# Two heads' key-value products in one chain of matmuls

## The chip, the cores and the metric

The kernel runs on one core of one Trainium2 chip. The metric is the device time of one execution in microseconds, from the median of several runs. The kernel before takes 1669.48 us (median of 3 runs, 1668.96 to 1672.15).

## What is computed

Linear attention with an RMS norm, and two MLPs behind it, all in float32 in and out. For each of 8 batches and 8 heads (576 positions, 64 channels):

```python
kv = np.einsum('bhsd,bhse->bhde', k, v)
out = np.einsum('bhsd,bhde->bhse', q, kv)
rms = np.sqrt(np.mean(out * out, axis=-1, keepdims=True) + 1e-06)
attn = out / rms * g_norm
x = attn.transpose(0, 2, 1, 3).reshape(4608, 512)
h = x @ moe_w_in;   x = np.where(h >= 1, h, np.where(h <= -1, 0, (h + 1)**2 / 4)) @ moe_w_out
h = x @ moe2_w_in;  x = np.maximum(h, 0)**2 @ moe2_w_out
```

The MLPs are 512 to 2048 to 512 wide. The change is in the first line alone: the product of the keys with the values, a 64 x 64 matrix for each head, summed over 576 positions.

## The kernel before

The work goes in blocks of 512 tokens. TensorE's product of two float32 numbers split in a high and a low part (three matmuls in the float32r format, `mm3`, L190) makes both MLPs accurate; the first MLP runs over 9 blocks of 16 hidden slices (`h_stage`, `g_stage`, `out_stage`), the second works on pairs of blocks with fewer products (L688), from about 850 us on. The main loop is a list of steps, one for each hidden slice; a table of hooks puts other work between the halves of a step: the loads and splits of the first MLP's weights during block 0, and the attention of the batch that the next block needs (`attention`, `load_kv`, `load_q`). Batch 0's attention runs ahead of all MLP work. The program's builder orders the queues of the engines from this; the order on an engine isn't always the code's.

The heads are taken in pairs, 4 pairs for each batch, 32 in all. For a pair, `load_kv` brings 512 of the 576 positions of the keys and of the values into a tile of 128 partitions x 512 numbers each: partition p holds positions 4p to 4p + 3 (L342 to L347). Both tiles are laid out head by head, so that the four positions of one head and one partition are one run of 1 KB. The last 64 positions of each head, the rest, go into a tile of their own with 64 partitions (L349, L350 for batches 1 to 7; for batch 0 all heads at once, L382). All these loads are issued by SyncE (SP), in one queue, together with those of queries, weights and outputs.

`kv_stage` (L388 on) then multiplies: for head 0 four float32 matmuls over 128 positions each and one over the rest, accumulated in one bank in rows and columns 0 to 63; then the same for head 1 in rows and columns 64 to 127. A float32 matmul is issued to TensorE as two pairs of a weight load and a matmul, so a pair of heads takes 20 matmul instructions: 16 of L395 (128 rows, 64 columns of weights, 64 columns moved) and 4 of L396 (64 rows). The bank's two diagonal blocks are then copied out, for batch 0 into `kv0`, otherwise split into `kvbd` (DVE, L171 and L404), block diagonal matrices whose other blocks stay zero. `o_stage` multiplies the transposed queries of both heads with them at once.

Of the kernel before, what the change touches and what calls it, by code (L numbers as in the profile page):

```python
# [73 lines left out]
def linear_attention_rms_two_mlps(  # L74
# [12 lines left out]
    nc = tc.nc  # L87
    B, H, S, D = q.shape
    NT, DM = out.shape
    DFF = w_in1.shape[1] // 2  # L90
    P = 128
# [4 lines left out]
    MR = TB // P  # L96
# [59 lines left out]
    def engine(op, phase):  # L156
        return engines[next(turns[op][min(phase, 2)])]
# [9 lines left out]
    def copy(e, dst, src):  # L167
        if e is nc.scalar:
            e.copy(dst, src)  # L169
        elif e is nc.vector:  # L170
            e.tensor_copy(dst, src)  # L171
        else:
            scaled(e, dst, src, 1.0)
# [149 lines left out]
    def bank(b, name):  # L323

        pool, tag = next(banks) if b == 0 else (ps_t, "at")
        return pool.tile([P, TB], F32, tag=tag, name=name)
# [9 lines left out]
    def load_kv(b, hp):  # L336
        h0 = 2 * hp
        if b > 0:
            r = ap2.tile([REM, 2, 2, D], F32, tag="rem", name=f"rem_{b}_{hp}")
            kvr[b, hp] = (r[:, 0], r[:, 1])  # L340
        for n, src in enumerate((k, v)):
            pool, tag = (ep, "e") if (b, hp) == (0, NP - 1) else (st, "st")  # L342
            t = pool.tile([P, TB], F32, tag=tag, name=f"{'kv'[n]}_{b}_{hp}")
            t = t.rearrange("p (h r d) -> p h r d", h=2, r=MR)
            rows = src[b, h0 : h0 + 2, :TB, :].rearrange("h (p r) d -> p h r d", r=MR)
            nc.sync.dma_start(t, rows)
            kvm.setdefault((b, hp), []).append(t)  # L347
            if b > 0:
                rest = src[b, h0 : h0 + 2, TB:, :].rearrange("h p d -> p h d")  # L349
                nc.sync.dma_start(kvr[b, hp][n], rest)  # L350
# [14 lines left out]
    def load_first():  # L365

        left = wp.tile([REM, 2, H, D], F32, tag="w0_3", name="kvr0")
        qr = wp.tile([REM, H, D], F32, tag="w1_3", name="qr0")
        for hp in range(NP):
            load_kv(0, hp)  # L370
            heads = slice(2 * hp, 2 * hp + 2)
            kvr[0, hp] = (left[:, 0, heads, :], left[:, 1, heads, :])
            pool, tag = (ep, "e") if hp == NP - 1 else (st, "st")
            t = pool.tile([P, TB], F32, tag=tag, name=f"q_0_{hp}")
            t = t.rearrange("p (c h d) -> p c h d", h=2, c=MR)
            for j in range(2):
                rows = q[0, 2 * hp + j, :TB, :].rearrange("(c p) d -> p c d", p=P)
                nc.sync.dma_start(t[:, :, j, :], rows)
            qs[0, hp] = [t[:, c] for c in range(MR)] + [qr[:, heads, :]]
            if hp == 0:  # L380
                for t, src in ((left[:, 0], k), (left[:, 1], v), (qr, q)):
                    nc.sync.dma_start(t, src[0, :, TB:, :].rearrange("h p d -> p h d"))  # L382
                for j in range(2):
                    nc.sync.dma_start(
                        gvec[j * D : (j + 1) * D, :], g_norm.rearrange("(d o) -> d o", o=1)
                    )

    def kv_stage(b, hp):  # L388
        kt, vt = kvm.pop((b, hp))
        r = kvr.pop((b, hp))  # L390
        ps = bank(b, f"pkv_{b}_{hp}")
        for j in range(2):
            s = slice(j * D, (j + 1) * D)
            for c in range(MR):
                nc.tensor.matmul(ps[s, s], kt[:, j, c, :], vt[:, j, c, :], start=c == 0, stop=False)  # L395
            nc.tensor.matmul(ps[s, s], r[0][:, j, :], r[1][:, j, :], start=False, stop=True)  # L396
        for j in range(2):
            s = slice(j * D, (j + 1) * D)
            if b == 0:
                copy(engine("kv_hi", b), kv0[s, hp, s], ps[s, s])  # L400
                continue
            t = kvbd[hp % len(kvbd)]
            copy(engine("kv_hi", b), t[s, 0, s], ps[s, s])
            nc.vector.tensor_tensor(t[s, 1, s], ps[s, s], t[s, 0, s].bitcast(F32), ALU.subtract)  # L404
# [73 lines left out]
    def attention(b):  # L478

        slots = {}  # L480

        def at(s, f, *a):
            slots.setdefault(s, []).append((f, a))

        def begin():
            new_x(1, b)
            xrem[b] = ap2.tile([P, KD, REM], F32, tag="xrem", name=f"xrem_{b}")

        at(0, begin)
        for hp in range(NP):  # L490
            for half in range(2):
                u = 2 * hp + half
                if half == 0:
                    at(6 * hp if b == 0 else 3 * u, kv_stage, b, hp)
                at(6 * hp if b == 0 else 3 * u, t_stage, b, hp, half)
                at(6 * hp + 5 if b == 0 else 3 * u + 2, o_stage, b, hp, half)
                at(6 * hp + 10 if b == 0 else 3 * u + 4, r_stage, b, hp, half)
        return slots
# [348 lines left out]
    for n, (L, b) in enumerate(blocks):  # L847
        nxt = blocks[n + 1] if n + 1 < len(blocks) else None
        if nxt and nxt[0] == 1 and nxt[1] < B:
            nb = nxt[1]  # L850
            for hp in range(NP):
                s = max(0, 6 * hp - 6)
                if hp > 0:
                    when = (n, s // 2)
                else:
                    when = (n, 0) if n == 0 else (n - 1, NF - 3)
                hook(*when, 0, load_kv, nb, hp)
                hook(*when, 0, load_q, nb, hp)
            hook(n, 0, 0, store_xrem, nb - 1)
            for s, fs in attention(nb).items():  # L860
                for f, a in fs:
                    hook(n, s // 2, s % 2, f, *a)
        elif nxt:
            hook(n, 0, 0, store_xrem, B - 1)
            for c in range(KD):
                hook(n, 2 + c, 0, load_x, *nxt, c)
                hook(n, 8 + c, 0, split_x, *nxt, c)
# [45 lines left out]
    ps = bank(0, "pwarm")  # L913
# [4 lines left out]
    for j in range(2):  # L918
        s = slice(j * D, (j + 1) * D)
# [100 lines left out]
```

## Time and profile before

| | |
|---|---|
| median of the runs | 1669.48 us |
| the profiled execution's own time | 1670.26 us |
| its span, first to last instruction | 1668.5 us |
| PE, matmuls | 1634.9 us busy, 98% |
| DVE, ACT | 61%, 56% busy |
| granted TensorE clock, mean of the span | 0.989 |
| DMA | 302 MB, 181 GB/s |
| instructions in the span | 21700 |

Engines are PE (TensorE's matmuls), PEld (its weight loads, which overlap PE), DVE (VectorE), ACT (ScalarE), POOL (GpSimd) and SP (SyncE, which issues the DMAs). Times in the rows are microseconds from the start of the span, if nothing else is said. Matmuls are pipelined: the shown length of one runs from its start to the modelled arrival of its last result, so that the next one begins before it ends. What a chain of matmuls costs is therefore read from start to start. L12 is line 12 of the kernel. "A <-B" behind an idle time names what ended it.

### The profile page before, as it was taken

Reading aid. Unit: us, or ns where it says so; the run is one execution under the profiler, and the core shown is the slowest. Engines: PE = TensorE matmul, PEld = TensorE weight load, DVE = VectorE, ACT = ScalarE, POOL = GpSimd, SP = SyncE. Lnnn points to the kernel's source line nnn. Section 1 sums busy time; section 2 is a strip of 40 time slices with the busy share of each in tenths; the row PEclk is TensorE's granted clock in tenths of the full one; section 3 lists DMA queues with packets and bytes.
Section 4 is the critical chain, followed back from the end, with each engine's and each line's share of the span. In section 5 each row is a group of like instructions: output and inputs, shape, how many; then the busy total and the mean of one; then the engine's idle time right before and its main releaser. Section 6 shows DMA issues by size and latency. Waiting matters only on the chain.

```text
span 1668.5 us, 21700 instructions
## 1 busy us (share of the span) xinstructions
PE 1634.9 (98%) x7640; PEld 1335.9 (80%) x7640; DVE 1009.6 (61%) x1846; ACT 936.6 (56%) x1757; POOL 111.9 (7%) x109
## 2 busy tenths in 40 slices
PE   7888999999999999999999999999999999999998
PEld 4666888888888888888888888888888878887886
DVE  5988775767767676653234346844874496447522
ACT  6775765657657565654344366545654664664321
POOL 0000000000000000000000022003101210230000
PEclk8998999999999999999999999999999999999999
DMA  8634747567574665704041356666756666665663
GB/s 258 211 121 139 239 142 240 177 185 249 163 239 148 209 188 154 242 1 155 1 138 52 113 191 225 206 222 199 241 193 224 196 236 212 207 220 188 220 195 108
DMA packets 219483, 302.37 MB, mean 181 GB/s; under 512 B 95728, under 2 KB 157168, under 8 KB 219376
## 3 DMA queue, kind: packets, MB, share of 16 engines
q1 hardware_dynamic: 219376, 301.00, 56.6%
q8 instruction: 61, 1.00, 0.2%
q14 instruction: 46, 0.38, 0.1%
HBM read 231.74 MB, written 69.21 MB: 180 GB/s over the span
## 4 chain that ended last, share of the span: by engine, by line
PE 89%; DVE 6%; ACT 2%; issue 1%; DMA 1%; SPq 0%; DVEq 0%; ACTq 0%
PE ph L190 26%; PE acc L190 25%; PE ph L688 18%; PE po L688 13%; PE pkv L395 2%; DVE t L633 2%; PE po L190 1%; PE pkv L396 1%; PE pr L454 1%; PE pt L835 1%; DMA xr<-x1d 1%; DVE x L633 1%; ACT w L169 0%; DVE d L222 0%; DVE h L741 0%
## 5 line engine op out<-in xcount | busy, mean ns | idle before, releaser
L190 PE MATMUL ph<-x,w 128*128 128x512 f32 x1728 | 427.7, 396 | 15.1 <-ACT w L169 8.5
L190 PEld LDWEIGHTS ph<-x,w 128*128 128x128 f32 x1728 | 325.7, 191 | 84.0 <-ACT w L169 12.5
L688 PE MATMUL po<-t,ws 128*128 128x512 f32 x1344 | 311.8, 391 | 2.4 <-DVE t L633 2.4
L688 PE MATMUL ph<-x,ws 128*128 128x512 f32 x1344 | 309.1, 390 | 0.0
L688 PEld LDWEIGHTS po<-t,ws 128*128 128x128 f32 x1344 | 250.2, 188 | 56.8 <-DVE t L633 5.6
L688 PEld LDWEIGHTS ph<-x,ws 128*128 128x128 f32 x1344 | 251.4, 188 | 51.9
L190 PE MATMUL acc<-gs,w 128*128 128x512 f32 x1152 | 284.9, 393 | 0.9 <-DVE gs L183 0.9
L190 PEld LDWEIGHTS acc<-gs,w 128*128 128x128 f32 x1152 | 212.1, 189 | 43.7 <-DVE gs L183 1.4
L523 ACT ACTIVATE u<-ph,halfb 128x512 f32<-128x512 f32 x144 | 99.2, 689 | 190.8 <-PE ph L190 190.3
L633 DVE TENSOR_TENSOR t<-g,t 128x512 fp32r<-128x512 f32 x192 | 134.8, 709 | 72.7 <-ACT t L169 72.7
L525 DVE SCALAR_TENSOR_TENSOR u<-u,ph 128x512 f32<-128x512 f32 x144 | 97.7, 679 | 125.9 <-ACT u L177 124.7
L169 ACT CAST t<-g 128x512 fp32r<-128x512 f32 x192 | 116.5, 621 | 72.3 <-DVE t L633 50.9
L169 ACT CAST gs<-u 128x512 fp32r<-128x512 f32 x160 | 99.4, 621 | 84.6 <-DVE u L525 72.6
L183 DVE TENSOR_TENSOR gs<-u,gs 128x512 fp32r<-128x512 f32 x160 | 110.2, 689 | 50.5 <-ACT gs L169 48.7
L190 PE MATMUL acc<-gs,wt 128*128 128x512 f32 x576 | 139.3, 391 | 0.0
L190 PEld LDWEIGHTS acc<-gs,wt 128*128 128x128 f32 x576 | 107.4, 188 | 22.4
L741 DVE TENSOR_TENSOR h<-ph,e 128x512 f32<-128x512 f32 x96 | 66.4, 691 | 63.2 <-PE ph L688 53.0
L177 ACT ACTIVATE u<-u 128x512 f32<-128x512 f32 x144 | 91.0, 633 | 1.7
L742 ACT ACTIVATE h<-h 128x512 f32<-128x512 f32 x96 | 60.7, 632 | 53.7 <-DVE h L741 48.8
L749 POOL TENSOR_TENSOR t<-g 128x512 f32<-128x512 f32 x32 | 43.1, 1347 | 649.6 <-ACT g L743 398.0
L743 ACT ACTIVATE g<-h 128x512 f32<-128x512 f32 x128 | 80.9, 632 | 3.6
L733 DVE TENSOR_TENSOR e<-ph,e 128x512 f32<-128x512 f32 x64 | 43.4, 688 | 47.0 <-PE ph L688 46.0
(101 smaller groups left out, 1619.6 us busy)
## 6 DMA issues: line engine op xcount, KB each, us to landing
ws<-wsd SPq DMA_DIRECT2D x224, 512.0 KB, 3.9
wsd<-s SPq DMA_DIRECT2D x112, 256.0 KB, 3.6
wt<-wtd SPq DMA_DIRECT2D x48, 512.0 KB, 4.0
raw<-in_moe_w_in_dram SPq DMA_DIRECT2D x32, 512.0 KB, 6.1
raw<-in_moe_w_out_dram SPq DMA_DIRECT2D x32, 512.0 KB, 5.6
wcd<-s SPq DMA_DIRECT2D x32, 512.0 KB, 3.5
ws<-wcd SPq DMA_DIRECT2D x32, 512.0 KB, 4.2
x1d<-ev SPq DMA_DIRECT2D x36, 256.0 KB, 3.6
```

What stands on the lines that cost most here:

```text
L169: e.copy(dst, src)
L177: e.activation(dst, src, AF.Square)
L183: engine(op + "_lo", phase).tensor_tensor(t[:, 1, :], src, t[:, 0, :].bitcast(F32), ALU.subtract)
L190: nc.tensor.matmul(dst, wt(a), xt(c), start=first and n == 0, stop=last and n == 2)
L523: nc.scalar.activation(u, ps, AF.Relu, bias=halfb, scale=0.5)
L525: nc.vector.scalar_tensor_tensor(u, u, 1.0, ps, op0=ALU.min, op1=ALU.max)
L633: engine2(op + "_lo").tensor_tensor(t[:, 1, :], src, t[:, 0, :].bitcast(F32), ALU.subtract)
L688: nc.tensor.matmul(ps, wt(a), xt(c), start=first and n == 0 and i == 0, stop=last and n == len(lhs) - 1 and i == 2, skip_group_check=True,)
L733: nc.vector.tensor_tensor(e[i, p], bank, e[i, 1], ALU.add)
L741: nc.vector.tensor_tensor(h, bank, add, ALU.add)
L742: nc.scalar.activation(h, h, AF.Relu)
L743: nc.scalar.activation(g, h, AF.Square)
```

## The change

The keys of a pair are laid side by side, position by position: for each of the four positions of a partition, the 64 channels of head 0 and then those of head 1. This is done by two DMAs for each key tile, one for each head, whose runs are 256 bytes instead of 1 KB. The values stay as they were and are read across both heads (two runs of 64 numbers) by the matmul. One chain of four matmuls over 128 positions and one over the rest then makes a 128 x 128 product: the two wanted blocks on the diagonal and, off it, the products of one head's keys with the other's values, which nothing reads. A pair takes 10 matmul instructions of 128 columns in place of 20 of 64. The copies out of the bank are the same.

```diff
         for n, src in enumerate((k, v)):
             pool, tag = (ep, "e") if (b, hp) == (0, NP - 1) else (st, "st")
             t = pool.tile([P, TB], F32, tag=tag, name=f"{'kv'[n]}_{b}_{hp}")
-            t = t.rearrange("p (h r d) -> p h r d", h=2, r=MR)
             rows = src[b, h0 : h0 + 2, :TB, :].rearrange("h (p r) d -> p h r d", r=MR)
-            nc.sync.dma_start(t, rows)
+            if n == 0:
+
+                t = t.rearrange("p (r h d) -> p r h d", h=2, r=MR)
+                for j in range(2):
+                    nc.sync.dma_start(t[:, :, j, :], rows[:, j])
+            else:
+                t = t.rearrange("p (h r d) -> p h r d", h=2, r=MR)
+                nc.sync.dma_start(t, rows)
...
         ps = bank(b, f"pkv_{b}_{hp}")
-        for j in range(2):
-            s = slice(j * D, (j + 1) * D)
-            for c in range(MR):
-                nc.tensor.matmul(ps[s, s], kt[:, j, c, :], vt[:, j, c, :], start=c == 0, stop=False)
-            nc.tensor.matmul(ps[s, s], r[0][:, j, :], r[1][:, j, :], start=False, stop=True)
+
+
+        kv = ps[:, :P]
+        for c in range(MR):
+            nc.tensor.matmul(kv, kt[:, c], vt[:, :, c, :], start=c == 0, stop=False)
+        nc.tensor.matmul(kv, r[0], r[1], start=False, stop=True)
```

## Rows read from the trace of the kernel before

**Rows 1.** The page, busy time, share of the span and instructions of the engines.

```profile
PE 1634.9 (98%) x7640; PEld 1335.9 (80%) x7640; DVE 1009.6 (61%) x1846; ACT 936.6 (56%) x1757; POOL 111.9 (7%) x109
```

**Rows 2.** Stretches: length, busy time of PE, PEld, DVE, ACT, POOL; clock, DMA share, GB/s.

```profile
4.70:26.00 21.30, 19.34 (x122) 13.41 (x121) 5.27 (x17) 11.60 (x31) 0.42 (x2) 0.84 0.92 279
26.00:47.00 21.00, 12.87 (x41) 8.13 (x40) 20.79 (x48) 19.28 (x45) 2.70 (x6) 0.83 0.83 238
47.00:158.00 111.00, 97.36 (x454) 74.74 (x454) 98.71 (x206) 75.98 (x155) 2.57 (x4) 0.93 0.49 151
158.00:736.00 578.00, 578.00 (x2892) 476.58 (x2893) 399.60 (x841) 368.01 (x753) 7.84 (x25) 1.00 0.61 189
```

**Rows 3.** The same for tile pkv alone: PE, PEld, DVE; clock, DMA share, GB/s.

```profile
158.00:736.00 578.00, 41.32 (x460) 33.50 (x460) 21.19 (x96) 1.00 0.61 189
```

**Rows 4.** What PE waited for: us in total, times, longest; the first of the list.

```profile
PE ph L190 <- ACT w L169: 8.5, 3, 3.0
```

**Rows 5.** Tiles pkv and rem: ns min/median/max, first and last start, shapes.

```profile
L395 PEld LDWEIGHTS pkv<-v,k x512: 132/138/231, 4.7 to 728.6; 128*64 128x64 f32 x171
L395 PE MATMUL pkv<-v,k x512: 222/222/369, 4.7 to 728.7; 128*64 128x64 f32 x171
...
L396 PE MATMUL pkv<-rem x112: 218/267/366, 48.2 to 729.0; 64*64 64x64 f32 x112
```

**Rows 6.** PE in order of time around the last product: start, length, what.

```profile
727.07 0.39 PE L190 MATMUL ph<-x,w 128*128 128x512 f32 x1
727.38 0.68 PE L395 MATMUL pkv<-v,k 128*64 128x64 f32 x8
727.99 0.33 PE L396 MATMUL pkv<-rem 64*64 64x64 f32 x2
728.25 0.68 PE L395 MATMUL pkv<-v,k 128*64 128x64 f32 x8
728.86 0.32 PE L396 MATMUL pkv<-rem 64*64 64x64 f32 x2
729.11 0.50 PE L190 MATMUL acc<-gs,w 128*128 128x512 f32 x1
```

**Rows 7.** PE in order of time around transposes: at 1092 us, and at 25.6 us.

```profile
1092.03 0.62 PE L688 MATMUL po<-t,ws 128*128 128x512 f32 x2
1092.49 0.60 PE L835 MATMUL pt<-ident,g 128*128 128x128 f32 x4
...
25.60 0.44 PE L414 MATMUL pt<-ident,q 128*128 128x128 f32 x2
25.97 0.24 PE L416 MATMUL pt<-ident,qr 32*128 32x32 f32 x1
```

**Rows 8.** The weight loads of head 0 of the last product, in order of time.

```profile
727.38 0.54 PEld L395 LDWEIGHTS pkv<-v,k 128*64 128x64 f32 x8 [0.35 <-issue]
```

**Rows 9.** PE in order of time at the start (4 to 9 us).

```profile
4.71 1.07 PE L395 MATMUL pkv<-v,k 128*64 128x64 f32 x8
6.43 0.52 PE L414 MATMUL pt<-ident,q 128*128 128x128 f32 x3 [0.65 <-DMA q<-in_q_dram]
7.27 0.29 PE L396 MATMUL pkv<-kvr 64*64 64x64 f32 x2 [0.32 <-DMA kvr<-in_v_dram]
...
8.36 0.33 PE L414 MATMUL pt<-ident,q 128*128 128x128 f32 x1
```

**Rows 10.** DMA issues: times, KB each, median us from issue to landing.

```profile
k<-in_k_dram SPq DMA_DIRECT2D x32, 256.0 KB, 4.2
...
q<-in_q_dram SPq DMA_DIRECT2D x8, 128.0 KB, 4.1
```

**Rows 11.** SP's issues of values (first pair, fifth pair), and PE's use of the fifth.

```profile
1.24 0.45 SPq L346 DMA_DIRECT2D v<-in_v_dram  x1
...
33.41 0.59 SPq L346 DMA_DIRECT2D v<-in_v_dram  x1
...
47.16 1.12 PE L395 MATMUL pkv<-v,k 128*64 128x64 f32 x8
```

## The prediction

> **What bounds the kernel now.** I read four views in this order: the page's busy shares, the busy time by stretches of time, the list of what TensorE waited for, and the order in time around one stage of the keys' product. On the page PE is busy 98% of the span [rows 1]; a busy PE can still be waiting inside its pipeline, so this only says where to look. The stretches say more [rows 2]. From 158 to 736 us PE is busy for 578.00 of 578 us at a granted clock of 1.00, while DVE is busy for 399.60 and ACT for 368.01. There TensorE sets the pace, and a microsecond less of PE is a microsecond less of time. From 47 to 158 us it is otherwise: PE has 97.36 of 111 us, DVE 98.71, and the longest waits of PE are for ACT's split of the first MLP's weights [rows 4]. From 26 to 47 us DVE has 20.79 of 21.00. From 4.7 to 26 us PE works 19.34 of 21.30 in a chain with little beside it. Of the 32 products of a pair (20 PE instructions each: a float32 matmul is issued as two), 23 stand in the PE-bound stretch (460 instructions) [rows 3]; four are batch 0's, before 26 us, and the other 5 lie in the DVE-bound stretch.
>
> **What one product costs now.** One 64-column instruction is shown with a median of 222 ns [rows 5], but they overlap; the price is the distance between starts. In the last product [rows 6] the last matmul of the hidden layer starts at 727.07, the first of head 0 at 727.38, its rest (64 rows) at 727.99, head 1 at 728.25, its rest at 728.86, the next work at 729.11. So 0.31 + 0.61 + 0.26 + 0.61 + 0.25 = 2.04 us. Inside a chain the weight loads follow each other at (0.54 - 0.14)/7 = 0.058 us [rows 5, 8], and the matmuls keep that pace: seven steps make 0.40 of the 0.61, so the remaining 0.2 lies in the change to the 64-row shape and in the first step. Each of the five changes of shape (full array to 64 columns, 64 columns to 64 rows by 64 columns and back, twice, and out) costs some 0.09 us beyond the work of the instruction before (0.31 against the 0.23 found below).
>
> **What it costs after.** One chain: eight instructions of 128 columns, two of 64 rows, and two changes of shape.
> - Into the chain: both shapes are the full array. The nearest row goes from 512-column matmuls to 128-column float32 transposes: the last of two starts at 1092.03 + 0.62 - 0.39 = 1092.26, the transposes at 1092.49, so 0.23 [rows 7].
> - Seven steps inside: the four transposes take 0.60 with 0.27 for one, so (0.60 - 0.27)/3 = 0.11 each [rows 7]; 7 x 0.109 = 0.76.
> - Chain to rest: the nearest row is the full-array transpose followed by a 32-row one. The second transpose starts at 25.60 + 0.44 - 0.27 = 25.77, the short one at 25.97: 0.20 [rows 7].
> - Rest, first to second: now 0.33 - 0.22 = 0.11 (two of them in [rows 6], less the shortest one of [rows 5]), with a load of 64 columns in the open. Twice the columns: 0.21, an estimate; 0.11 if that load is hidden.
> - Rest to the next work: now 0.25 - 0.11 = 0.14; 64 more columns at 0.053 make 0.20.
>
> Sum 0.23 + 0.76 + 0.20 + 0.21 + 0.20 = 1.60, a gain of **0.44 us** for each product. Bounds: 1.50 with the rest's load hidden (gain 0.54); 1.80 if the first load stays open as now (0.31 and one step of 0.21) and a step is 0.112 (gain 0.24). No row shows a moving operand in two runs of 64, which is how the values are now read; I take it at the price of one run, since its columns are as many, and put its upper bound into the first rival.
>
> **Where it counts.** In the PE-bound stretch all of it: 23 x 0.44 = **10.1 us** (5.5 to 12.4 by the bounds). From 47 to 158 us PE often waits, so I count half of 5 x 0.44, **1.1 us** (0 to 2.2). The clock there averages 0.93 [rows 2], that is 0.07 x 111 / 0.5 = 15.5 us at the lower level of 1.2 GHz, and it fell after PE had idled; a stretch more or less of a third of that is 5 us at half speed, so another 2.6 us either way.
>
> In batch 0 the first product must wait for its rest, which lands at 7.27; the second head's chain then follows, and the next work starts at 8.36 [rows 9], 1.09 later. With one chain all but the rest is done by then: 0.21 + 0.20 = 0.41 remains. Against it, the rest stands one DMA issue further back on SP's queue: 0.45 us by the issue of the values [rows 11], 0.5 as an estimate with the gap behind it. Net 0.2. The other three at 0.44 make 1.3; together **1.5 us**.
>
> **The keys' DMA.** Each key load of 256 KB in runs of 1 KB becomes two of 128 KB in runs of 256 bytes. The first queries go exactly like this: 128 KB, 4.1 us to landing, against 4.2 for a key load [rows 10]. SP issues 32 more transfers at about 0.5 us, 16 us of its queue over 736 us. Queued behind each are the values, the rests and the queries of the same pair. I cost this at nothing outside the start: the tightest pair after batch 0 has its values issued at 33.41 and used at 47.16 [rows 11], 13.7 us for a landing of about 4, and half a microsecond more leaves 9. If that cover were gone, PE would wait by what is late. At the start it isn't nothing: four more issues put the first raw weights 2.0 us later, with the DMA engines 0.92 busy [rows 2]. DVE is busy without a gap from 26 to 47, so the weights were there in time; I take 0, and +2.0 as the other end. The product's wait for a further semaphore costs nothing while the loads land that early. PSUM now also gets the two blocks off the diagonal; the copies read the same 64 x 64 blocks, so DVE does what it did.
>
> **Sum:** 1670.26 - 10.1 - 1.1 - 1.5 = 1657.6 for the profiled execution (its span 1668.5 and 1.8 around it). It lies 0.78 above the median of 1669.48, so the forecast for the median is **1656.8 us**.
>
> **Rivals.** *The weight loads come into the open* (slower). Now a load of 64 columns and a pass over 64 columns share one step of 0.058. If loads of 128 columns don't hide behind passes of 128 columns in the same rows, a step is some 0.21 (the 0.11 that the rest's second step takes with its load in the open, doubled) instead of 0.109: seven steps add 0.71 and the entry 0.08, so 2.39 us against 2.04, +0.35, and 23 of them make 8.1: 1678 us. A doubled read of the two-run operand would cost the same. It decides from a step of 0.109 + 0.44/7 = 0.172 on. Against it stand the steps of rows 7 and 8, where loads do hide; for it only that those are transposes or half as wide. The Trainium skill (TensorE: Matmul & The Clock Gate, Part 3, The mechanism) says that a weight load overlaps a running matmul only when the row group differs. By that rule a step is the load plus the pass; the trace disagrees for 64 columns at 0.058 [rows 8]. I give this rival 0.05.
>
> *The start loses what the products gain.* The keys' longer way through SP and through busy DMA engines delays the first weights, and DVE's unbroken work from 26 us on shifts with them by the 2.0 us above, doubled if the split weights and one half-clock stretch follow: 1669.5 - 10.1 + 4 = 1663.4. For it: the queue is full up to 26 us. Against it: DVE starts that work when PE's fourth product is done, which comes earlier. 0.11. The Trainium skill (DMA: Bandwidth & Descriptors, Specifications) asks for at least 512 bytes in a transfer for line rate, which speaks against runs of 256. The trace's 4.1 us against 4.2 for twice the bytes agrees that such runs are slower per byte.
>
> *Nothing comes of it.* The order on PE isn't the code's (three transposes stand between head 0's chain and its rest at the start [rows 9]), so the builder may order the shorter product differently, and PE may wait where it now doesn't: 0.44 us of wait at each product gives 1669. Against it: no wait of PE at all from 158 to 736. 0.04.
>
> **Numbers.** Forecast 0.80, with a range of its own of 1652 to 1663 (the bounds of the 23 alone give 1654.5 to 1661.4; the start and the middle widen it). The second rival lies inside 1651 to 1664, so that is the range. A measurement here can tell about 0.2%, 3.3 us, from no change. Faster: 0.80 + 0.11 = 0.91; the same 0.04; slower 0.05.
>
> **What would show it.** Right: the keys' matmuls at half their number (256 of 128 columns, 64 of the rest), 0.11 us from start to start, about 1.6 us from the last hidden matmul to the next work, and PE still without a gap between the end of the weights' split and the second MLP, that stretch being about 10 us shorter. Wrong: steps of 0.17 us or more; waits of PE for the keys' DMA; a start (up to the first dense PE work) that is longer than now.

## The result and the profile after

The changed kernel takes 1648.92 us (median of 4 runs, 1647.81 to 1650.88), against 1670.82 for the kernel before in the same session (4 runs): a ratio of **0.987 [0.9853, 0.9887]**, a gain of 21.9 us. Two later sessions gave 0.9881 [0.9861, 0.9901] and 0.9888 [0.9872, 0.9905], gains of 19.2 and 20.1. The forecast was a gain of 12.7, and its range ended at 1651.0. The sign was right, the size was not.

Busy time on the page of the changed kernel, and its DMA line (answers to [rows 1]):

```profile
PE 1618.8 (98%) x7320; PEld 1329.3 (81%) x7320; DVE 1005.3 (61%) x1846; ACT 936.4 (57%) x1757; POOL 114.2 (7%) x109
DMA packets 244568, 302.33 MB, mean 183 GB/s; under 512 B 129008, under 2 KB 182256, under 8 KB 244464
```

PE has 320 instructions fewer and 16.1 us less of busy time. Busy time isn't time of the path, so the stretches come next, in the columns of [rows 2]; the last line is tile pkv alone, as in [rows 3]:

```profile
4.70:26.00 21.30, 19.54 (x81) 14.21 (x81) 6.75 (x20) 12.08 (x32) 0.63 (x3) 1.00 0.93 256
26.00:47.00 21.00, 15.49 (x52) 9.44 (x49) 19.85 (x45) 19.06 (x44) 5.57 (x5) 0.84 0.89 265
47.00:158.00 111.00, 97.53 (x428) 76.44 (x428) 103.72 (x217) 79.62 (x160) 2.54 (x4) 0.97 0.53 160
158.00:736.00 578.00, 578.00 (x2716) 482.24 (x2715) 399.97 (x848) 375.80 (x773) 7.38 (x26) 1.00 0.62 189
...
158.00:736.00 578.00, 33.74 (x230) 30.82 (x230) 20.19 (x92) 1.00 0.62 189
```

After 158 us TensorE is still busy without a gap, and there the change does what was forecast. What is new stands in the third line: DVE now does 103.72 us of work between 47 and 158 us, where it did 98.71. The first MLP's weights are split sooner.

The clock of 1.00 in the first line misleads. The clock's records of this execution begin at 16.6 us, and the column counts the time before them as full speed. The distances between matmuls show the lower level until then: the eight instructions of the first product take 2.05 us (its row at 5.54 us is shown further down), those of the last product 1.05. It is so in all 18 traces: up to the first record the matmuls are as far apart as at the lower level.

PE's waits between 47 and 158 us have changed as well (the first two of the list for this stretch; before, 8.5 us for ACT's cast [rows 4] and 4.1 for the same work of DVE):

```profile
PE ph L190 <- DVE u L532: 5.5, 3, 2.3
PE ph L190 <- ACT w L169: 5.5, 2, 2.8
```

The last product of the changed kernel on PE, in order of time (answers to [rows 6]):

```profile
706.29 2.43 PE L190 MATMUL ph<-x,w 128*128 128x512 f32 x10
708.55 1.05 PE L402 MATMUL pkv<-v,k 128*128 128x128 f32 x8
709.54 0.48 PE L403 MATMUL pkv<-rem 64*128 64x128 f32 x2
709.95 1.43 PE L190 MATMUL acc<-gs,w 128*128 128x512 f32 x5
```

The last hidden matmul starts at 706.29 + 2.43 - 0.39 = 708.33, the next work at 709.95: **1.62 us** for a product, forecast 1.60, before 2.04. A step inside the chain takes (1.05 - 0.275)/7 = 0.111 us with 0.275 for one instruction. The rest's second instruction starts 0.48 - 0.27 = 0.21 us behind its first, with 0.27 for its own length, and the next work 0.20 us behind that.

**Three parts of the span.** DVE's first and last subtraction in a weight split (tile w) cut the span into the start, the stretch in which the first MLP's weights are made (DVE is busy for 112 to 114 us in it, in every kernel), and the rest, which is bound by PE. The table gives them for all kernels, one profiled execution each; "low" is the time of the middle part at TensorE's lower level of 1.2 GHz in the clock's records.

| kernel | median us | ratio to before | start | middle | low | rest |
|---|---|---|---|---|---|---|
| before | 1670.82 | | 31.9 | 125.7 | 23.9 | 1510.8 |
| changed | 1648.92 | 0.987 | 31.9 | 116.3 | 10.2 | 1500.9 |
| changed, second session (e10) | 1651.20 | 0.9881 | 30.1 | 118.1 | 13.6 | 1502.3 |
| changed, third session (e16) | 1650.07 | 0.9888 | 30.6 | 116.3 | 10.2 | 1501.2 |
| e1 keys' DMA alone | 1674.23 | 1.0031 | 36.7 | 123.8 | 13.7 | 1510.2 |
| e2 batches 0 to 2 | 1658.32 | 0.9940 | 29.2 | 116.5 | 10.2 | 1509.3 |
| e3 batches 3 to 7 | 1662.13 | 0.9953 | 36.2 | 121.3 | 10.2 | 1503.1 |
| e4 all, padded to the old length | 1660.53 | 0.9949 | 32.7 | 114.6 | 3.4 | 1509.7 |
| e5 before, PE kept busy at the start | 1663.48 | 0.9968 | 30.9 | 121.9 | 13.7 | 1510.4 |
| e6 changed, one warm-up matmul | 1652.66 | 0.9893 | 34.0 | 116.3 | 6.8 | 1500.6 |
| e7 batch 0 | 1666.55 | 0.9973 | 29.9 | 121.6 | 13.2 | 1511.5 |
| e8 batches 1 and 2 | 1662.09 | 0.9946 | 36.0 | 118.7 | 13.7 | 1507.2 |
| e9 before, 14 matmuls more in the middle | 1671.14 | 0.9998 | 34.6 | 125.9 | 20.5 | 1510.1 |
| e11 changed, a key half issued by ACT | 1649.46 | 0.9875 | 31.6 | 122.2 | 13.7 | 1497.0 |
| e12 batches 1 to 7, start as e5 | 1648.60 | 0.9875 | 30.8 | 121.1 | 20.5 | 1499.8 |
| e13 before, five products shortened | 1667.24 | 0.9979 | 35.9 | 120.9 | 13.7 | 1510.4 |
| e14 the same, start as e5 | 1663.95 | 0.9961 | 31.3 | 121.9 | 20.5 | 1509.0 |
| e15 changed, five products lengthened | 1649.44 | 0.9882 | 33.5 | 115.1 | 3.4 | 1499.1 |

Read it by columns. **The rest** is 1507 to 1511.5 wherever batches 3 to 7 have products of the old length, and 1497 to 1503 wherever they don't. **The start** of the kernel before differs from execution to execution: the five kernels that have it unchanged show 31.9, 36.2, 36.0, 34.6 and 35.9, mean 34.9. The two executions compared first happen to have 31.9 both, which hides that the changed start is 31.1 in the mean of seven (changed, e2, e4, e7, e10, e15, e16). **The middle** falls with the time at the lower level, and beside that in two groups. The border between middle and rest moves with the order of the queues: in e11 the middle is as long as with the old products, but the rest is the shortest of all, and the two together, 1619.2, lie among those of the changed kernel (1617.2 to 1620.4).

### The profile page after: what moved, and what is told of

Read it like the earlier page. It is cut to its first block, busy times and chain, and to the rows that moved or that the text cites. A ratio compares the mean times of both kernels' runs of the same rounds, so it can differ in the third digit from the quotient of the medians.

```text
span 1649.1 us, 21087 instructions
## 1 busy us (share of the span) xinstructions
PE 1618.8 (98%) x7320; PEld 1329.3 (81%) x7320; DVE 1005.3 (61%) x1846; ACT 936.4 (57%) x1757; POOL 114.2 (7%) x109
## 4 chain that ended last, share of the span: by engine, by line
PE 88%; DVE 7%; ACT 2%; issue 1%; DMA 1%; SPq 0%; DVEq 0%; ACTq 0%
PE ph L190 26%; PE acc L190 25%; PE ph L695 18%; PE po L695 13%; DVE t L640 2%; PE pkv L402 2%; PE po L190 1%; PE pr L461 1%; DMA xr<-x1d 1%; PE pt L842 1%; PE pkv L403 1%; DVE w L183 1%; DVE x L640 1%; DVE d L222 1%; DVE d L225 0%
## 5 line engine op out<-in xcount | busy, mean ns | idle before, releaser
L190 PEld LDWEIGHTS ph<-x,w 128*128 128x128 f32 x1728 | 323.8, 190 | 81.8 <-ACT w L169 10.1
L532 DVE SCALAR_TENSOR_TENSOR u<-u,ph 128x512 f32<-128x512 f32 x144 | 97.8, 679 | 126.1 <-ACT u L177 125.5
L169 ACT CAST t<-g 128x512 fp32r<-128x512 f32 x192 | 116.5, 621 | 71.7 <-DVE t L640 50.1
```

The source lines that it names most:

```text
L190: nc.tensor.matmul(dst, wt(a), xt(c), start=first and n == 0, stop=last and n == 2)
L532: nc.vector.scalar_tensor_tensor(u, u, 1.0, ps, op0=ALU.min, op1=ALU.max)
```

## The experiments

### Which batches bring the gain, and what the keys' DMA costs alone (e1, e2, e3, e7, e8)

The change was made for some batches only (b < 3; b >= 3; b == 0; b in (1, 2)), and its DMA part alone, with the products read from the new layout as before:

```diff
-                nc.tensor.matmul(kv, kt[:, c], vt[:, :, c, :], start=c == 0, stop=False)
+                nc.tensor.matmul(ps[s, s], kt[:, c, j, :], vt[:, j, c, :], start=c == 0, stop=False)
...
-        kv = ps[:, :P]
+        if b >= 3:
+            kv = ps[:, :P]
```

> Only the keys' DMA is changed (two transfers, side by side); the products stay head by head in 64 columns. The work theory (every instruction time that TensorE saves counts in full, before 158 us as well, because VectorE's queue there hangs on TensorE's results) expects no gain: 1670 to 1673 us, the start some 1 to 2 us longer by the later queue of SP. The order theory (the builder puts the queues of the first block in another order once the loads or the products change, and this order and not the saved time shortened the stretch up to 158 us) expects a part of the head's 9.5 us already here: 1662 to 1668 us.

> Change made for batches 0 to 2 alone, 12 of the 32 products, 3 of them in the stretch where TensorE sets the pace. Both theories expect the head's gain of 9.5 us and 3 x 0.42 behind it: about 1660 us. If it is above 1665, the head's gain needs what the later batches do.

> Change made for batches 3 to 7 alone: 20 products, all in the stretch where TensorE is busy without a gap. 20 x 0.42 = 8.4 us: 1662.4 us, and the stretch up to 158 us as before, within 1 us.

> Change made for batch 0 alone, 4 of the 32 products. The clock theory expects the higher clock of the changed kernel (0.994 or more) and 1662 to 1666 us. If saved TensorE time is all: 4 x 0.42 = 1.7 us at most, less what the keys' later queue costs: 1668 to 1670 us.

> Change made for batches 1 and 2 alone, 8 products, 5 of them in the stretch where VectorE is the busier engine. Clock as before (0.989 to 0.991). If saved time counts in full there as well: 8 x 0.42 = 3.4 us, 1666 us; if it counts by half for the five: 2.3 us, 1667 us; if the order of the queues makes the difference: 1660 to 1664 us.

Measured: e1 1.0031 [1.0019, 1.0044]; e2 0.9940 [0.9924, 0.9956]; e3 0.9953 [0.9934, 0.9971]; e7 0.9973 [0.9963, 0.9983]; e8 0.9946 [0.9930, 0.9962]. Batches 3 to 7 (20 products) give 0.0047 of 1669.2, 7.8 us, and their rest is 7.7 us shorter than that of before: 0.39 us for each product, near the forecast's 0.44. Batch 0 gives 0.0027, 4.5 us, and batches 1 and 2 give 0.0054, 9.0 us. These are four and eight products; at 0.44 us they would be worth 1.8 and 3.5. Most of the gain that the forecast lacks is here. The three parts add up to 0.0128 against 0.0130 for the whole; e2 gives 0.0060, less than its two parts together (0.0081); the intervals allow that.

The DMAs alone are not free: +5.2 us (3.2 to 7.3). Only some of it can be placed: the middle is 1.9 us longer than e5's at the same 13.7 us of low clock, and the first product starts at 5.74 us behind the values, where e3's starts at 4.36.

### Is it the products' time? (e4, e9, e13, e14, e15)

e4 gives every product of the changed kernel its 0.44 us back: four more instructions of 128 columns ahead of the chain, whose result the chain overwrites.

```diff
         kv = ps[:, :P]
+        for i in range(2):
+            nc.tensor.matmul(kv, kt[:, 0], vt[:, :, 0, :], start=True, stop=True)
```

> The changed kernel with four more instructions of 128 columns in each product (two matmuls whose result is overwritten), 4 x 0.109 = 0.44 us, so that a product costs on TensorE what it cost before. The work theory expects the gain to go: 1669 to 1673 us. The order theory expects the head to keep most of its 9.5 us: 1661 to 1664 us.

Measured: 0.9949 [0.9934, 0.9965], 1660.53. The rest went back to 1509.7 and the median by 11.6 us (10.2 to 13.2 by the ratios, since the two medians are of different sessions). 0.0051 of 1669.2, 8.5 us, stayed a gain with products as long as before, so these don't come from shorter products. The middle stayed short as well. Some of this may be the added work's own doing: the profiled execution has 3.4 us of low clock in the middle, those of the changed kernel 10.2 and 13.6.

e9 puts 14 small matmuls between the hidden layer's chains of block 0 in the kernel before:

```diff
+        if L == 1 and b == 0 and f >= 2:
+            nc.tensor.matmul(ps[0:32, 0:4], ones[0:32, 0:32], xs[L, b][0][0:32, 0, 0:4], start=True, stop=True)
```

> The kernel before with 14 tiny matmuls of 32 rows put between the hidden-layer chains of batch 0, about 0.25 us each by the 32-row steps, 3.5 us of TensorE work in the stretch that is bound by DVE. Theory A (in that stretch TensorE's time is hidden, and what the changed products of batches 1 and 2 gave there came with the order of the queues): 1669 to 1670.5, the stretch between the first and the last weight split within 1 us of the 125.7 of before or of the 122 of the other kernels with unchanged products. Theory B (TensorE's time there counts, by way of ACT's casts that stand behind TensorE's results): 1673, the stretch 3 us longer. A mean clock other than .990 moves either by 1 us for each .001.

Measured: 0.9998 [0.9986, 1.0011], and a middle of 125.9 for 125.7 with 3.4 us less at the lower level (worth 1.1 by the rate found below). The 14 matmuls cost less than expected, though. Between two hidden chains one makes 0.33 + 0.12 us of the usual 0.23, 0.21 more, and five of the thirteen that fall in the middle stand behind a wait of PE, where they add some 0.1. So about 2.3 us were added there (an estimate from these starts), and at most 1.3 of them show.

e13 goes the other way: the five products of the middle are cut to a quarter of their main positions, with SP's order as before and 5 of DVE's 1846 rows moved. This leaves out most of those positions. e14 adds the busy start of e5.

```diff
-            for c in range(MR):
+            for c in range(1 if b == 1 or (b, hp) == (2, 0) else MR):
```

> The kernel before with the products of batch 1 and the first of batch 2 (the five in the stretch bound by DVE) over a quarter of their main positions: 12 matmuls of 0.058 us less in each, 0.70 us of TensorE, 3.5 us in all, with the queues of DVE, ACT and SP ordered as before. This leaves out part of those products. Theory A (TensorE's time is hidden in that stretch, the changed kernel's gain there came with the order of the queues and the clock): 1669 to 1671, the stretch between the first and last weight split as long as in the kernels with unchanged products at the same half-speed time (122 us at 13.7 us, 125.7 at 23.9). Theory B (TensorE's time there counts): 1666 to 1667, the stretch 3.5 us shorter than that.

> The same with the 8 filling matmuls that keep the clock up at the start. Theory A: 1663 to 1664, as the filling alone; theory B: 1660, 3.5 us less.

Measured: 0.9979 [0.9969, 0.9990] and 0.9961 [0.9947, 0.9975]. So theory A, that TensorE's time is wholly hidden there, falls for the old order: 3.5 us less of it gave 2.7 us by the medians of e13, 0.5 us the wrong way by the medians of e14 against e5 (1.2 us the right way by their ratios, which were taken in different sessions), and 1.0 us by the middles of e13 and e5 at the same low clock (121.9 to 120.9). It counts in part. The fifth product also moved on PE with the cut, which will matter below.

e15 adds twice the saving to the five products of the changed kernel (4 in place of e4's 2, in those five alone; SP's order unchanged, 15 of DVE's 1846 rows moved). e16 is the changed kernel beside it.

> The changed kernel with 8 more 128-column matmul instructions at 0.109 us, 0.87 us, ahead of each of the five products in the stretch bound by DVE: 4.4 us of TensorE, twice what the change saves there; their result is overwritten by the product. SP's queue is ordered as in the changed kernel, 26 rows of DVE's 1844 stand elsewhere. If TensorE's time counts there in part, as the shortened products showed (1 to 2.7 of 3.5 us): 1.2 to 3.4 us over the changed kernel, 1650.5 to 1654. If in full: 4.4 us over it, 1653.5 to 1655.5. If the gain there came with the order of the queues alone: no more than 1 us over it.

> The changed kernel for the same reference: 1648.5 to 1651.5.

Measured: e15 1649.44, 0.9882 [0.9868, 0.9897]; e16 1650.07, 0.9888 [0.9872, 0.9905]. **4.4 us more of TensorE cost nothing that can be measured.** Part of the reason is where they stand. Behind the first of the five products and behind the fifth PE waits for DVE, 1.45 and 2.30 us in the changed kernel's profile and 0.55 and 1.40 in e15's: there 1.8 of the 4.4 us fill time that was idle. The other three products are 0.83 to 0.89 us longer from their start to the next work, 2.6 us together. The windows show more; the middle part of each kernel in the columns of [rows 2], first the kernel before:

```profile
31.90:157.70 125.80, 106.98 (x480) 80.97 (x480) 113.43 (x239) 90.35 (x186) 4.45 (x8) 0.91 0.53 162
```

e3, with the same products and order in this part:

```profile
36.20:157.50 121.30, 101.92 (x480) 76.95 (x480) 113.06 (x239) 90.84 (x186) 4.47 (x8) 0.96 0.56 169
```

the changed kernel:

```profile
31.90:148.20 116.30, 100.63 (x430) 76.43 (x430) 112.58 (x237) 89.57 (x182) 7.90 (x8) 0.96 0.59 176
```

and e15:

```profile
33.50:148.60 115.10, 101.38 (x470) 79.28 (x470) 112.39 (x238) 88.70 (x182) 7.92 (x8) 0.99 0.59 177
```

DVE's work is 112.4 to 113.4 us in all of them, so the length of this part is that work and DVE's waits. Between the first two lines order and products are the same and the clock goes from 0.91 to 0.96: 125.8 to 121.3 us. By the low times of the table that is (125.7 - 121.3)/(23.9 - 10.2) = 0.32 us for each microsecond at the lower level. The executions of the kernel before say the same: of 78 on record, the 14 with a mean clock of 0.986 or 0.987 took 1673.1 us in the mean, the 13 with 0.991 or 0.992 took 1668.3. That is 4.8 us for 0.0044 of the clock, or 14.8 us at half speed: 0.32 for each. The second and the third line have the same clock, and differ by 5.0 us. In e15's profile the clock stands at 0.99, and that pays for the added work: 6.8 us less of low clock at 0.32 is 2.2, the middle is shorter by 1.2, so the 4.4 us, of which 2.6 stand in the way, cost 1.0. That the added work raised the clock is not shown: this is one execution, and the mean clocks of e15's four, 0.994 to 0.998, are those of the changed kernel's (0.994 to 0.998 in three sessions).

DVE's waits in these windows (us in total, times, longest), for the kernel before, the changed kernel and e15:

```profile
DVE w L183 <- ACT w L169: 10.1, 8, 2.1
```

```profile
DVE w L183 <- ACT w L169: 2.9, 6, 1.0
```

```profile
DVE w L183 <- ACT w L169: 1.9, 6, 0.5
```

One kind of wait makes the difference: DVE's second half of a weight split waits for ACT's cast. ACT's cast itself needs no matmul, but it stands in ACT's queue behind the activation of a hidden slice, which waits for PE. The 23rd weight in the kernel before, ACT and then DVE in order of time:

```profile
119.41 0.69 ACT L523 ACTIVATE u<-ph,halfb 128x512 f32<-128x512 f32 x1 [1.97 <-PE ph L190]
119.99 0.65 ACT L161 ACTIVATE raw<-raw 128x512 f32<-128x512 f32 x1
120.54 0.60 ACT L169 CAST w<-d 128x512 fp32r<-128x512 f32 x1
...
119.11 0.42 DVE L221 TENSOR_SCALAR d<-raw 128x512 int32<-128x512 int32 x1
121.17 0.69 DVE L183 TENSOR_TENSOR w<-d,w 128x512 fp32r<-128x512 f32 x1 [1.65 <-ACT w L169]
```

The same weight in the changed kernel:

```profile
114.53 0.69 ACT L530 ACTIVATE u<-ph,halfb 128x512 f32<-128x512 f32 x1 [2.05 <-PE ph L190]
115.25 0.63 ACT L177 ACTIVATE u<-u 128x512 f32<-128x512 f32 x1
115.79 0.60 ACT L169 CAST w<-d 128x512 fp32r<-128x512 f32 x1
...
114.83 0.68 DVE L532 SCALAR_TENSOR_TENSOR u<-u,ph 128x512 f32<-128x512 f32 x1
116.42 0.69 DVE L183 TENSOR_TENSOR w<-d,w 128x512 fp32r<-128x512 f32 x1 [0.92 <-ACT w L169]
```

ACT waits for PE as long as before (2.05 us), and DVE loses 0.92 instead of 1.65, because its queue has another piece of work (L532) in the gap. The program's builder orders the queues anew when a product's instructions change: up to the last weight split, 38 of DVE's 277 rows and 47 of ACT's 228 stand elsewhere in the changed kernel's trace (the fewest that must be taken out so that the others have one order in both). Where the lower clock makes ACT's wait for PE longer, the same chain costs more; the kernel before loses most at the 27th weight, behind hidden matmuls that ran from 133.88 to 138.35 at the lower level:

```profile
138.38 0.69 ACT L523 ACTIVATE u<-ph,halfb 128x512 f32<-128x512 f32 x1 [2.34 <-PE ph L190]
138.97 0.61 ACT L169 CAST w<-d 128x512 fp32r<-128x512 f32 x1
...
139.61 0.69 DVE L183 TENSOR_TENSOR w<-d,w 128x512 fp32r<-128x512 f32 x1 [2.15 <-ACT w L169]
```

That weight has no wait in the changed kernel's first profile, and none in e3's either: its wait goes with the clock.

Does the order of the queues make the gain, then? Two runs come close to a test. Up to the last weight split, e7 has the middle's products as before, with queues nearer to the changed kernel's (11 of DVE's rows and 21 of ACT's stand elsewhere; 34 and 47 against the kernel before). e8 has the new products there, with queues nearer to those of the kernel before (19 and 21; 36 and 45 against the changed kernel). Their middles in the columns of [rows 2], behind that of e5, whose order and products are the old ones:

```profile
30.90:152.80 121.90, 102.95 (x480) 77.39 (x480) 113.07 (x239) 90.67 (x186) 4.46 (x8) 0.94 0.55 167
29.90:151.50 121.60, 104.73 (x480) 78.07 (x480) 112.48 (x238) 89.41 (x182) 7.91 (x8) 0.95 0.57 174
36.00:154.70 118.70, 100.34 (x430) 77.56 (x430) 113.00 (x239) 90.97 (x186) 4.41 (x8) 0.94 0.58 171
```

With nearly the same low clock (13.7, 13.2 and 13.7 us), e7 is as long as e5, and e8 is near the changed kernel's second session (118.1 at 13.6). The medians agree: e7's gain of 4.5 us is no more than its shorter start (29.9 for 34.9). So the gain in the middle went with the products and not with the order of DVE and ACT alone, by one profile of each. At single weights both count. At the 23rd, e7 has DVE's other work in the gap as the changed kernel has, and waits 0.86 us. At the 31st, e7 and e1 wait 1.53 and 1.61 us, like the kernel before, where the second half of the fifth product stands on PE inside the hidden slice that ACT waits for:

```profile
149.08 0.68 PE L395 MATMUL pkv<-v,k 128*64 128x64 f32 x8
152.31 0.69 ACT L523 ACTIVATE u<-ph,halfb 128x512 f32<-128x512 f32 x1 [2.08 <-PE ph L190]
...
154.20 0.69 DVE L183 TENSOR_TENSOR w<-d,w 128x512 fp32r<-128x512 f32 x1 [1.93 <-ACT w L169]
```

In the changed kernel the rest of that product stands behind the slice:

```profile
142.82 0.69 ACT L530 ACTIVATE u<-ph,halfb 128x512 f32<-128x512 f32 x1 [0.79 <-PE ph L190]
...
144.72 0.69 DVE L183 TENSOR_TENSOR w<-d,w 128x512 fp32r<-128x512 f32 x1 [0.23 <-ACT w L169]
...
145.34 0.38 PE L402 MATMUL pkv<-v,k 128*128 128x128 f32 x2
```

That the clock shortens the middle is shown (e3 against before, same order, and the 78 executions). The products' own time counts there in part: 1.0 of 3.5 us in e13, 1.0 of the 2.6 in e15, at most 1.3 of some 2.3 in e9, by single profiles; the medians allow from none (e15) to 2.7 of 3.5 (e13). Where the remaining 4 us come from is not shown. It is not the products' length alone (e4, e15), not the clock (equal), not the DMAs alone (e1's middle is no shorter), and not the order of DVE and ACT alone (e7, e8). The gain came where the products of batches 1 and 2 go in one chain. Whether it is the place that the builder then gives them on TensorE, as at the 31st weight, or something else about the single chain, no run separates.

### What happens at the start (e5, e6, e11, e12)

e5 is the kernel before with eight bf16 matmuls on zeros, four between the first head's chain and its rest and four a little later, where PE would wait for loads. The order of everything else is unchanged. On PE all eight stand together, from 5.76 to 8.16 us.

```diff
+    def keep_busy(n):
+        for i in range(n):
+            nc.tensor.matmul(pw, warm[:, :P], warm, start=True, stop=True)
...
+                if (b, hp, j) == (0, 0, 0):
+                    keep_busy(4)
...
+            if (hp, half) == (0, 1):
+                keep_busy(4)
```

> The kernel before, with eight more bfloat16 matmuls of 512 columns (0.21 us each at the upper clock level) on the warm-up tile between head 0's chain and its rest in the very first product, where TensorE otherwise waits for loads; no instruction of any engine changes its place otherwise. The clock theory (the part of the gain that was not forecast comes from TensorE's clock: with the first product in two chains TensorE idles at 5.8 to 7.3 us and the clock then falls for 7 us or more) expects a mean clock of 0.993 to 0.995 and 1663 to 1666 us. The theory that the saved time of the products alone counts expects 1669 to 1671 us: nothing is saved here.

e6 is the changed kernel with `WARM = 1` in place of 8.

> The changed kernel with one warm-up matmul in place of eight, every other instruction in its place. The clock theory expects the first products at the lower clock level, a mean clock of 0.988 to 0.992 and 1653 to 1657 us. Without an effect of the clock: 1648 to 1650 us.

Measured: e5 0.9968 [0.9956, 0.9980], 5.3 us **faster with more work**; e6 0.9893 [0.9877, 0.9909], with a start of 34.0 where the changed kernel has 30.1 to 31.9 (and e15, whose start is the same, 33.5). e6's 1652.66 lies between the two times expected, and its interval overlaps those of the changed kernel, so it shows little. The order being the same and the work more, e5's gain is the clock. From 9.5 to 29.2 us, in the columns of [rows 2], the kernel before:

```profile
9.50:29.20 19.70, 18.30 (x104) 12.26 (x105) 7.73 (x22) 13.40 (x36) 0.63 (x3) 0.84 0.93 288
```

e3, whose start is the kernel before's:

```profile
9.50:29.20 19.70, 18.71 (x89) 12.39 (x88) 4.84 (x15) 10.55 (x28) 0.42 (x2) 0.62 0.78 254
```

e5:

```profile
9.50:29.20 19.70, 17.37 (x112) 11.60 (x111) 9.43 (x27) 14.86 (x39) 0.73 (x4) 1.00 0.97 304
```

the changed kernel (e10; in the first profile of it the clock's records begin only at 16.6 us):

```profile
9.50:29.20 19.70, 15.72 (x78) 10.79 (x76) 10.74 (x30) 16.76 (x44) 0.84 (x4) 1.00 0.99 296
```

The clock in front is 0.84, 0.62, 1.00 and 1.00, and the first weight split comes at 31.9, 36.2, 30.9 and 30.1 us. With the old start PE works for 1 us and then waits twice for loads ([rows 9], 0.65 and 0.32; in e3 1.29 and 0.50), and the clock falls right behind that, at 9.0 us and 7.3 us, for 6.8 and 17.1 us. With the new one PE waits once, ahead of the first product, and then works for some 4 us (5.76 to 9.62 in e10). In e16, where it waited again at 6.76 and 7.97, the clock fell for 3.4 us at 11.7. But e13, with the old start, waited only 0.16 us for the queries and stayed at the lower level until its first record at 24.2 us. What raises and lowers the clock in the first 25 us is therefore not settled by waits alone. The start of the changed kernel on PE, in order of time (answers to [rows 9]):

```profile
5.54 2.05 PE L402 MATMUL pkv<-v,k 128*128 128x128 f32 x8 [0.76 <-DMA v<-in_v_dram]
7.38 1.06 PE L421 MATMUL pt<-ident,q 128*128 128x128 f32 x4
8.37 0.79 PE L403 MATMUL pkv<-kvr 64*128 64x128 f32 x2
```

The product waits 0.83 us longer for the values (5.54 for 4.71), which stand behind two key transfers, and its rest comes at 8.37 for 7.27. The chain takes 2.05 us here because the clock is at the lower level. In e16, at the upper level, it takes 1.13 and ends before the queries have landed, so that PE waits; the single chain does not remove the waits by itself.

The start is 3.8 us shorter in the mean (31.1 for 34.9), as short as the filled old start (30.9, 30.8, 31.3). Most of this is the clock. With the time up to the first record counted as low, the five old starts have 12.4 (before), 21.0 (e3), 20.9 (e8), 18.3 (e9) and 24.2 us (e13) of it, 19.4 in the mean; the seven changed ones 4.0 (e2) to 20.7 (e15), 11.6 in the mean; the filled ones 7.0 to 8.3. From before to e3 each microsecond of it makes the start 0.49 us longer, from e10 to e15 0.31. By these rates 7.8 us less are worth 2.4 to 3.8 us, an estimate that leaves 0 to 1.4 for the products' own time.

e12 has batch 0 as before with e5's filling, and the change for the others. e11 is the changed kernel with the second key half of batch 0 issued from ACT's queue:

```diff
-                    nc.sync.dma_start(t[:, :, j, :], rows[:, j])
+                    e = nc.scalar if b == 0 and j == 1 else nc.sync
+                    e.dma_start(t[:, :, j, :], rows[:, j])
```

> The changed kernel once more, so that it has the same reference as the next two: 1648 to 1650.

> The changed kernel with the second key half of batch 0 issued from ACT's queue, so that SP issues no more transfers at the start than before. If the start got no shorter because the values stand behind two key transfers, the first product begins 0.5 us earlier and the time is 1647 to 1648; if the DMA engines' own time is what the first product waits for, 1649 as without it.

> Batch 0 as before with the 8 filling matmuls of the run that kept TensorE busy at the start, the change for batches 1 to 7. If the parts add up (.0032 for the start's clock, .0054 for batches 1 and 2, .0047 for batches 3 to 7): ratio .987, 1647.5, as fast as the whole change, whose part in batch 0 is then worth no more than the clock that it keeps up. If the whole change saves work at the start too: 2 to 3 us slower than it.

Measured: e10 1651.20, 0.9881 [0.9861, 0.9901]; e11 1649.46, 0.9875 [0.9853, 0.9896]; e12 1648.60, 0.9875 [0.9855, 0.9896]. All three agree within their intervals. e12 says that, as far as intervals of some 3 us can tell, the change is worth no more in batch 0 than eight filling matmuls: what it brings there can be the clock alone. e11 didn't start sooner. Its values were issued at 1.50 us instead of 2.14 but landed at 6.44 instead of 5.40, as ACT issued the second halves of the next pairs' keys right with the first; the first product came at 6.53. So this run doesn't tell what the values' place in SP's queue costs. Nothing tried is measurably faster than the change itself.

## Why the prediction was wrong, point by point

- **One product, 2.04 to 1.60 us: right.** Measured 1.62 (0.23 to the chain for 0.23, 0.78 for 0.76 inside, 0.21 for 0.20 to the rest, 0.21 for 0.21 in the rest, 0.20 for 0.20 out), a gain of 0.42. The values' two runs of 64 cost nothing. The first rival fell: the step is 0.111 us, under its bound of 0.172. The sentence cited for that rival (the Trainium skill, TensorE: Matmul & The Clock Gate, Part 3, The mechanism) doesn't hold in this trace for loads of 128 columns in the same rows either.
- **23 products in the PE-bound part, 10.1 us: right.** At 0.42 they make 9.7; the rest is 1501.5 in the mean of the three changed profiles against 1510.4 in those of before, e5 and e9: 8.9.
- **"From 47 to 158 us PE often waits, so I count half of 5 x 0.44, 1.1 us", with the clock as "another 2.6 us either way": the step that failed most.** The middle is 6.8 us shorter in the mean (125.7, 125.9, 121.3 and 121.9 of before, e9, e3 and e5 give 123.7; 116.3, 118.1 and 116.3 give 116.9). The products' own part is some 0.6 to 1.1 (a quarter to a half of 5 x 0.42), no more than I counted. The clock makes 1.9 (17.1 us at the lower level in the mean of those four, 11.3 in the three, at 0.32). Some 4 are left; they came with the single chain in batches 1 and 2, and how is open. What failed is the price by PE's time alone. The forecast saw PE's waits for ACT's split and took PE as the one that matters; the row it had [rows 2] shows PE with 97.36 and DVE with 98.71 of 111 us, neither full. It did not ask what DVE waited for. DVE had 10.1 us of waits for ACT's casts in the middle, room for a gain (or a loss) that no PE row shows.
- **The start, 1.5 us from shorter products: too small, and without its main term.** The rest was taken to come 0.5 us later; in the profile it comes 1.10 later (8.37 for 7.27) and the first product 0.83, at the lower level. What came, 3.8 us in the mean and 4.5 by the runs with batch 0 alone, is mostly the clock (2.4 to 3.8 by the estimate above), which the forecast named only for the middle and as a risk of either sign; the products' time may be the remainder. That the clock alone can bring as much is shown (e5, e12). Why it stands higher with the single chain is not.
- **The keys' DMA at nothing, +2.0 as the other end.** Alone it costs 5.2 us (e1), more than that end. In the whole change this can't be taken apart from the clock and the order. The landing is as forecast: two transfers of 128 KB at 3.8 us in place of one of 256 KB at 4.2 [rows 10]:

```profile
k<-in_k_dram SPq DMA_DIRECT2D x64, 128.0 KB, 3.8
```

- **The second rival** (the start loses 4 us) had the right place and the wrong sign, and **the third** didn't come: PE still has no wait from 158 to 736 us.
- **The sum, with what was found:** 3.8 + 6.8 + 8.9 = 19.5 against gains of 21.9, 19.2 and 20.1. The forecast had 1.5 + 1.1 + 10.1. The range took the clock's 2.6 us as its only allowance for the middle and none for the order; with 4 us more for what the profile of before didn't price there, its lower end would have been 1647.

## What to carry to other kernels

In a part where no engine is full, look at what each engine waits for and through whose queue, before pricing a saving by the engine that is to be relieved; a wait behind another engine's queue can be worth more than the saving. Count the clock as a term of its own: in the start of this kernel it was worth more than the instructions that the edit removed, and filling a wait of TensorE with matmuls on zeros is a cheap way to find that out. Look at where the clock's records begin before trusting a mean of them. Where a program is ordered by a builder, every edit also draws a new order, so that an edit of the work and its order come together; here 4 us stayed unexplained between them. One profile of each kernel (31.9 us for both starts) was not enough to see what was systematic.

## What the runs showed of the hardware that was not expected

More TensorE work made the kernel faster: eight matmuls on zeros in the gaps of the start gave 5.3 us (e5). In the middle 4.4 us of added work cost nothing that can be measured (e15), 1.8 of them in time that PE spent waiting. A step of 0.111 us holds a weight load of 128 columns and a pass of 128 columns in the same rows, about twice the 0.058 us of 64 columns [rows 5, 8], and the rest's second instruction comes 0.21 us behind its first, twice its old 0.11. In all 18 traces the clock's records begin where the steps first fall to those of the upper level, 3.8 to 24.2 us into the span.
